# A transformer block on one Trainium2 core: weight parts in two of five pairs of scores instead of two of three

## The chip, the cores and the metric

The kernel runs on one core of one Trainium2 chip. The time is the device time of one execution in microseconds (us); where several runs are told of, it is their median. The engines are PE (matrix multiplication; PEld is its weight load), ACT (exponentials and other functions), DVE (vector work), POOL (GpSimd) and SP, which here only issues transfers. Each engine carries out its own instructions in the order of the program and waits where an instruction needs something that is not there yet.

## The reference

The block takes 2048 tokens of width 512, with 32 heads of width 16 that share one key and one value head, and a gated feed-forward part of width 1792, all in float32.

```python
q = (layernorm(x) @ wq) as 32 heads;  k = layernorm(x) @ wk;  v = layernorm(x) @ wv
h = x + concat_heads(softmax(q k^T / 4) v) @ wo
out = h + (gelu(layernorm(h) @ w_gate) * (layernorm(h) @ w_up)) @ w_down
```

## The kernel before, in words

Accuracy comes from splitting: each float32 matrix is held as a high part and a low part, and a product is three matrix products. The weights `wo`, `w_gate`, `w_up` and `w_down` are split once, during the attention, and the two parts go to DRAM, from where the feed-forward part loads them for each of the four blocks of 512 tokens.

**The scores.** Attention runs over the 4 blocks of tokens; a block has 8 groups of 4 heads, and a group has 16 chunks of 128 keys. For one chunk of one group there are two *scores* (`scores`, L382, called by `score`, L1008): each is two matmuls (L394) into one PSUM tile and one exponential on ACT over 128x1024 (L398). The program counts scores with `n`: 32 to a group, 256 to a block. Two scores with even and odd `n` make a pair; each pair also lets `weigh` (L400) multiply an earlier chunk's exponentials with the values (L402) into the accumulator `acc` of the group. When a group is done, `evacuate` (L413) copies `acc` to `oT` on DVE (L415), SP stores it to DRAM (L419, `acc_d`), and loads it back in another order (L428, `oc`); DVE inverts and multiplies it (L442, L445) and splits it (L453, L457). The queries of the next group are loaded by SP from `q_d` (L374, `qg`) once the current group is at its third chunk.

**Block 0** is written by hand in a loop of its own: `while n < 2 * KC` (L1044) for the first group, `n` from 0 to 31, and `while n < lead` (L1056) for the rest, `n` from 32 to 271, two scores a turn. It has two side works. The first is the queries of the rest of block 0 and of blocks 1 to 3 (`project_q`, L187, called through `later_q`, L306): two or four half matmuls (L392) go beside the scores of a pair; when a group of 128 query columns is done, DVE takes it out of PSUM (L119, L120; a short copy `mark`, L210, stands between its two halves), and SP stores it to `q_d` (L245, three transfers). After four of these the bound of the scores follows: DVE takes the largest norm (L260, L261, into `q`), POOL works out two factors (`factors`, L265: four small operations into `mm`, L266 to L275) two turns later, DVE makes `m` from them (L282) two turns after that, and SP stores `m` (L286).

**The weight parts** are the second side work (`part_weights`, L489, a generator with 46 steps: 4 of `wo`, then for each of 14 columns one of `w_gate`, one of `w_up` and one of `w_down`). I number them 0 to 45. A step issues, in this order: the store of the part before it (POOL's queue, L508 or L514, 512 KB), the load of the part three ahead (SP's queue, L497, 256 KB, into one of four buffers `raw`), and on POOL the split of its own part (`part_f`, L500: a cast, L119, and a subtraction, L120, both over 128x512; for `w_down` a multiplication, L503, ahead of them) into one of two buffers `both`. So a cast waits for its load and for the store of the part two before it, and a load waits until POOL has done with the part four before the one that is loaded.

The engines PE, POOL, ACT, SP and DVE all keep the order in which the program issues here. That order decides what an SP transfer or a POOL operation stands behind. Steps 0 to 3 are taken in the first group (L1052). All others are taken at L1094, at the end of a turn.

At `n` = 256 the loop takes what is left of the weight parts (L1067), closes the buffers of the early stage, and loads `wo` on POOL's queue (L564). From `n` = 272 on the feed-forward work of block 0 is woven between the scores of block 1, and so on; the last block's comes behind all scores.

Of the kernel before, what the change touches and what calls it, by code (L numbers as in the profile page):

```python
# [52 lines left out]
def kernel(  # L53
# [96 lines left out]
    def attend(first):  # L150
        with ExitStack() as outer:
            with tc.manual_schedule(
                engines={mybir.EngineType.PE, mybir.EngineType.Pool, mybir.EngineType.Activation}
            ):
                run(outer, first)


    def run(outer, first):
# [147 lines left out]
        def later_q():  # L306

            second = project_q(1, range(DC), nc.vector, 1, (0, 1))
            for _ in range(sum(RAMP.values())):
                yield next(second)  # L310

            next(q_rest)
            for _ in range(2 * DC - sum(RAMP.values())):
                yield next(second)
            yield from q_rest
            yield 0
            yield from second
            for b in range(2, NB):
                yield from project_q(b, range(DC), nc.vector, b, ())

        def age():
            for entry in after:
                entry[0] -= 1
            while after and after[0][0] <= 0:
                after.pop(0)[1]()
# [83 lines left out]
        def take_out():  # L409
            for step in outs.pop(0):  # L410
                step()
# [148 lines left out]
        def load_wo(b):  # L560

            for j in range(DC // 2):
                w = db.tile([P, 2, 2, D], F32R, tag="w2", bufs=W2, name=f"wo_{b}_{j}")
                (nc.sync if b else nc.gpsimd).dma_start(  # L564
                    w.bitcast(F32),
                    wo_d[2 * j : 2 * j + 2].rearrange("c p i d -> p c i d").bitcast(F32),
                )
                wos[b, 2 * j], wos[b, 2 * j + 1] = w[:, 0], w[:, 1]
# [416 lines left out]
        def finish(n):  # L985
            for _ in range(min(n, len(pend))):
                pb, pg, pkc, pp, pacc, _ = pend.pop(0)
                weigh(pacc, pp, pkc)
                if pkc == KC - 1:
                    evacuate(pb, pg, pacc)  # L990
# [17 lines left out]
        def score(n, beside=()):  # L1008

            nonlocal acc  # L1010
            i, u = divmod(n, 2)
            b, r = divmod(i, PER)
            g, kc = divmod(r, KC)
            if u == 0:
                if kc == 0:
                    cur["qg"] = qgs.pop((b, g))
                    acc = pss.tile([P, T], F32, tag="acc", bufs=1, name=f"acc_{b}_{g}")
                if kc == 2 and b * NG + g + 1 < NB * NG:
                    key = divmod(b * NG + g + 1, NG)
                    qgs[key] = load_q(*key)  # L1020
                cur["p"] = sb.tile([P, 4, T], F32, tag="p", bufs=PB, name=f"p_{i}")
            scores(i, cur["p"], cur["qg"], kc, u, beside)
            if u == 1:
                pend.append((b, g, kc, cur["p"], acc, n))
# [12 lines left out]
        n, lead = 0, 2 * PER + sum(SIZES[: LEAD[0]])  # L1037
        with tc.manual_schedule(engines={mybir.EngineType.SP, mybir.EngineType.DVE}):
            parts, said = None, 3 if first else 0
            if first:  # L1040
                work = later_q()
                parts = part_weights(early.enter_context(tc.tile_pool(name="parts", bufs=1)))

            while n < 2 * KC:  # L1044
                for _ in range(RAMP.get(n, n > 7 and n % 4 == 3) if said else 0):
                    said = next(work)
                    age()
                score(n)
                n += 1
                if n % 4 == 0:  # L1050
                    finish(len(pend) - 2)
                    if parts is not None and n > 12 and n % 24:  # L1052
                        next(parts)

            token, left = next(work) if first else None, 6 * (NB * DC - 2 - DC) * DC
            while n < lead:  # L1056
                age()
                rest = token == REST
                count = 0
                if token is not None and not rest:  # L1060
                    count = min(4 if left > LAST_Q - n else 2, token[1] + 1)
                    left -= count
                if n == 2 * PER:
                    assert token is None
                    while after:
                        age()
                    for _ in parts or ():  # L1067
                        pass
                    if first:
                        check_bound(eb, k2m)  # L1070
                    parts = work = None
                    early.close()
                    db = late.enter_context(tc.tile_pool(name="dense", bufs=1))
                    load_wo(0)
                for j in range(2):
                    if j >= 2 - count // 2:
                        tokens = token, next(work)
                        score(n, [(lane, step) for lane, _, step in tokens])
                        token = next(work, None)
                    else:  # L1080
                        score(n)
                    n += 1
                if n == 2 * PER + 4:
                    primed = dense(0)
                    next(primed)
                if rest:
                    token = next(work, None)
                if len(pend) > 2:
                    finish(1)
                while squares:  # L1090
                    squares.pop(0)()
                if outs and n % 4 == 0:
                    take_out()
                if parts is not None and n % 6:  # L1094
                    next(parts, None)
            assert n == lead
        assert not outs
# [339 lines left out]
    def check_bound(sb, k2m):  # L1437
        q2m = sb.tile([H, 1], F32, name="q2m")
        nc.vector.tensor_reduce(q2m, q2, axis=AX.X, op=ALU.max)
        nc.vector.tensor_tensor(q2m, q2m, k2m, op=ALU.mult)  # L1440
        nc.sync.dma_start(b_d.rearrange("o h -> h o"), q2m)
# [77 lines left out]
```

## Time and profile before

| | us |
|---|---|
| median of 3 runs (lowest, highest) | 1479.35 (1477.3, 1481.3) |
| the profiled execution's own time | 1478.19 |
| its span | 1476.5 |
| PE busy | 1407.0 (95%) |
| ACT busy | 1045.6 (71%) |
| DVE busy | 542.4 (37%) |
| POOL busy | 200.5 (14%) |
| mean granted clock of PE | 0.98 |

How to read it: the profile is one execution. A strip of 40 digits shows the busy tenths of 40 equal slices of the span, 36.9 us each. A timeline merges neighbouring instructions of one kind into a row: start, duration, engine, line, what is written from what, how many (x), and in brackets the idle time ahead of it and what ended that. A table by stretches gives the busy time of each engine between two times, the granted clock of PE and the mean share of the transfer engines that was busy. Rows of SP are issues of transfers, not the transfers themselves.

### The profile page before, as it was taken

The numbers are of one execution on the slowest core, as the hardware profiler recorded it, in microseconds if no ns is written. First come the engines' busy times: TensorE is split into PE (matmuls) and PEld (weight loads), VectorE is DVE, ScalarE is ACT, GpSimd is POOL, SyncE is SP. The second block draws the span as 40 slices with busy tenths as digits, with TensorE's granted clock in tenths as the row PEclk, the third lists the DMA queues.
The fourth block names the chain that finished last, engine by engine and source line by source line (L and its number), as shares of the span: only waits on it lengthen the run. The fifth ranks groups of instructions, "written<-read, shape, count | busy, mean of one in ns | idle before, by whom it ended". The sixth has DMA issues, their size and how long they took to land.

```text
span 1476.5 us, 25577 instructions
## 1 busy us (share of the span) xinstructions
PE 1407.0 (95%) x10622; PEld 778.5 (53%) x10622; DVE 542.4 (37%) x974; ACT 1045.6 (71%) x1149; POOL 200.5 (14%) x286
## 2 busy tenths in 40 slices
PE   9997972899999999999999999999999999999998
PEld 7532320233456565555555555555555555557886
DVE  7411310221345243343334242422344242426665
ACT  7696962799778777777777777777778777773000
POOL 6267766300000000000000000000000000002000
PEclk9998986899999999999999999999999999999999
DMA  4577777424224223223334142405144131426462
GB/s 152 170 230 232 242 228 236 147 80 150 78 79 145 102 97 126 83 83 110 113 102 148 60 155 69 140 27 183 41 162 139 40 133 58 155 91 216 164 211 70
DMA packets 84700, 193.69 MB, mean 131 GB/s; under 512 B 9676, under 2 KB 24012, under 8 KB 84544
## 3 DMA queue, kind: packets, MB, share of 16 engines
q1 hardware_dynamic: 77208, 165.65, 33.6%
q0 software_dynamic: 7200, 26.22, 4.6%
q8 instruction: 85, 1.39, 0.4%
q14 instruction: 39, 0.32, 0.1%
q10 hardware_dynamic: 168, 0.10, 0.0%
HBM read 142.12 MB, written 49.55 MB: 130 GB/s over the span
## 4 chain that ended last, share of the span: by engine, by line
PE 78%; DMA 10%; POOL 5%; ACT 3%; issue 2%; DVE 1%; SPq 1%; POOLq 0%; DVEq 0%; ACTq 0%
PE acc L402 26%; PE s L394 16%; PE pu L913 8%; PE pg L913 7%; PE pd L913 4%; PE pd L590 3%; PE pd L612 3%; PE pg L612 3%; PE pu L612 3%; ACT p L398 2%; DMA w_d<-w_0b 2%; PE pp L590 2%; DMA w_d<-w_1b 1%; POOL w_1b L120 1%; PE pp L721 1%
## 5 line engine op out<-in xcount | busy, mean ns | idle before, releaser
L398 ACT ACTIVATE p<-s 128x1024 f32<-128x1024 f32 x1024 | 974.1, 1029 | 288.4 <-PE s L394 286.7
L402 PE MATMUL acc<-p,v_sb 128*32 128x512 f32 x4096 | 500.9, 602 | 8.9 <-DVE oT L415 8.9
L394 PE MATMUL s<-qg,kaug 50*128 50x512 f32 x1984 | 423.6, 429 | 11.8 <-DMA qg<-q_d 8.1
L394 PEld LDWEIGHTS s<-qg,kaug 50*128 50x128 f32 x1984 | 192.8, 185 | 267.6 <-ACT p L398 157.8
L402 PEld LDWEIGHTS acc<-p,v_sb 128*32 128x32 f32 x4096 | 107.9, 109 | 235.5 <-issue 221.5
L913 PE MATMUL pg<-x2h,w 64*128 64x512 f32 x672 | 211.5, 391 | 0.9 <-DVE mark_pg L936 0.9
L913 PE MATMUL pu<-x2h,w 64*128 64x512 f32 x672 | 212.2, 391 | 0.0
L913 PEld LDWEIGHTS pg<-x2h,w 64*128 64x128 f32 x672 | 116.0, 185 | 15.2 <-DVE mark_pg L936 1.8
L913 PEld LDWEIGHTS pu<-x2h,w 64*128 64x128 f32 x672 | 115.8, 185 | 15.3
L913 PE MATMUL pu<-x2l,w 64*128 64x512 f32 x336 | 121.9, 391 | 0.0
L913 PE MATMUL pg<-x2l,w 64*128 64x512 f32 x336 | 121.9, 390 | 0.0
L790 ACT ACTIVATE ga<-ga 128x512 f32<-128x512 f32 x56 | 35.3, 634 | 89.2 <-DVE ga L785 89.2
L129 POOL TENSOR_SCALAR rstd<-mv 128x1 f32<-128x1 f32 x16 | 3.6, 222 | 682.6 <-DVE mv L127 682.6
L913 PE MATMUL pd<-w,gh 64*128 64x512 f32 x384 | 81.2, 392 | 0.0
L855 DVE TENSOR_TENSOR h<-h,pd 128x512 f32<-128x512 f32 x48 | 31.9, 684 | 115.4 <-PE pd L913 66.3
L442 DVE RECIPROCAL oc<-oc 128x128 f32<-128x128 f32 x64 | 56.3, 921 | 47.9 <-DMA oc<-acc_d 43.3
L1146 DVE SCALAR_TENSOR_TENSOR ga<-ga,g 128x512 f32<-128x512 f32 x70 | 48.3, 690 | 52.6 <-ACT ga L790 51.5
L392 PE MATMUL pq<-xT_hi,wq_hi 64*128 64x512 f32 x80 | 33.6, 419 | 34.6 <-DVE mark L210 33.7
L774 DVE COPY g<-pg 128x512 f32<-128x512 f32 x56 | 38.7, 692 | 63.9 <-PE pg L913 58.2
L913 PEld LDWEIGHTS pu<-x2l,w 64*128 64x128 f32 x336 | 57.9, 185 | 7.4
L913 PEld LDWEIGHTS pg<-x2l,w 64*128 64x128 f32 x336 | 58.0, 185 | 6.9
L415 DVE COPY oT<-acc 128x512 f32<-128x512 f32 x32 | 22.1, 691 | 97.6 <-PE acc L402 97.4
(258 smaller groups left out, 1451.5 us busy)
## 6 DMA issues: line engine op xcount, KB each, us to landing
w<-w_d SPq DMA_DIRECT2D x112, 512.0 KB
w<-w_d SPq DMA_DIRECT2D x28, 1024.0 KB
qg<-q_d SPq DMA_DIRECT2D x48, 200.0 KB
q_d<-qh SPq DMA_DIRECT2D x32, 256.0 KB
acc_d<-oT SPq DMA_DIRECT2D x31, 256.0 KB
oc<-acc_d SPq DMA_DIRECT2D x124, 64.0 KB
w_d<-w_0b POOLq DMA_DIRECT2D x14, 512.0 KB, 6.1
w_d<-w_1b POOLq DMA_DIRECT2D x14, 512.0 KB, 4.8
```

Of the source, the lines that this page charges most:

```text
L392: step()
L394: nc.tensor.matmul(s[:, a, :], kaug[rows, kc * P : (kc + 1) * P], qg[rows, 2 * u + a, :], start=True, stop=True,)
L398: nc.scalar.activation(p[:, 2 * u : 2 * u + 2, :], s, AF.Exp, scale=SCALE)
L402: nc.tensor.matmul(acc[32 * j : 32 * j + 32, :], v_sb[:, kc, :], p[:, j, :], start=(kc == 0), stop=(kc == KC - 1), skip_group_check=True,)
L442: nc.vector.reciprocal(oc[:, 1, sl], oc[:, 1, sl])
L590: nc.tensor.matmul(banks[k], lhsT[rows], rhs[rows], start=(turn == 0 and i == 0), stop=(turn == 1 and i == n - 1), skip_group_check=True,)
L612: nc.tensor.matmul(bank, lhsT, rhs, start=(i == 0), stop=(i == len(ts) - 1))
L774: nc.vector.tensor_copy(g, pg)
L790: nc.scalar.activation(a, a, AF.Tanh, scale=GELU_A * GELU_C)
L855: nc.vector.tensor_tensor(hs[t], hs[t], pd, op=ALU.add)
L913: nc.tensor.matmul(e["bank"], lhsT[rows], rhs[rows], start=i == 0 and not e["both"], stop=last and e["both"], skip_group_check=True,)
L1146: (soon or lazy).pop(0)()
```

## The change

One line is changed, in the loop that issues scores 32 to 271 (L1094):

```diff
-                if parts is not None and n % 6:
+                if parts is not None and n // 2 % 5 in (0, 2):
                     next(parts, None)
```

`n` is even there. Before, a step was taken in every turn whose `n` is no multiple of 6, two turns of three: step 4 at `n` = 34, steps 5 and 6 at 38 and 40, 7 and 8 at 44 and 46, and so on to step 45 at `n` = 158; the last store follows at 160. Now a step is taken in two turns of five: step 4 at `n` = 34, 5 and 6 at 40 and 44, 7 and 8 at 50 and 54, and so on to step 45 at `n` = 240; the last store follows at 244.

The instructions of PE, ACT and DVE are the same and in the same order. On POOL the weight parts and their stores keep their order, and two sets of four `mm` operations stand at other places among them: the set of block 1 now stands behind the split of part 9 (before: 12), that of block 2 behind the split of part 26 (before: 42). That of block 3 still stands behind the last part. On SP the weight loads move back among the stores to `q_d`, `m` and `acc_d` and the loads `oc` and `qg`: the last one, of part 45, now stands just ahead of the store of group 6's `acc` (counted from 0), where before it stood ahead of group 4's. Ahead of the store of group 2's `acc` stand the loads up to part 19; before it were those up to part 28.

## The prediction

> **What bounds the kernel now.** I read the strips of the page first. (Differences under 0.3% of the time, 4.4 us, count as no change here: about what a measurement of this kernel can tell.)
>
> ```profile
> PE   9997972899999999999999999999999999999998
> POOL 6267766300000000000000000000000000002000
> PEclk9998986899999999999999999999999999999999
> ```
>
> PE is busy from end to end, except in slices 3, 5 and 6 (111 to 258 us), and these lie in block 0, in the stretch where POOL splits the weights. The clock falls there too. Next, ACT's timeline through block 0. It holds the scores alone, so the x counts give `n`: the first row is `n` = 32, the second 66, the last 242.
>
> ```profile
> 85.63 1.94 ACT L398 ACTIVATE p<-s 128x1024 f32<-128x1024 f32 x2 [0.43 <-PE s L394]
> ...
> 122.73 3.86 ACT L398 ACTIVATE p<-s 128x1024 f32<-128x1024 f32 x4 [0.20 <-PE s L394]
> 135.97 1.94 ACT L398 ACTIVATE p<-s 128x1024 f32<-128x1024 f32 x2 [9.38 <-PE s L394]
> 138.53 24.77 ACT L398 ACTIVATE p<-s 128x1024 f32<-128x1024 f32 x26 [0.62 <-PE s L394]
> ...
> 202.29 1.94 ACT L398 ACTIVATE p<-s 128x1024 f32<-128x1024 f32 x2 [9.18 <-PE s L394]
> 205.73 15.21 ACT L398 ACTIVATE p<-s 128x1024 f32<-128x1024 f32 x16 [1.51 <-PE s L394]
> 221.72 10.49 ACT L398 ACTIVATE p<-s 128x1024 f32<-128x1024 f32 x11 [0.78 <-PE s L394]
> 266.07 1.03 ACT L398 ACTIVATE p<-s 128x1024 f32<-128x1024 f32 x1 [33.86 <-PE s L394]
> 268.72 1.94 ACT L398 ACTIVATE p<-s 128x1024 f32<-128x1024 f32 x2 [1.62 <-PE s L394]
> 271.77 9.27 ACT L398 ACTIVATE p<-s 128x1024 f32<-128x1024 f32 x10 [1.11 <-PE s L394]
> ...
> 350.73 22.11 ACT L398 ACTIVATE p<-s 128x1024 f32<-128x1024 f32 x24 [0.55 <-PE s L394]
> ```
>
> Three standstills are to be seen, at `n` = 70, 128 and 157: 9.38, 9.18 and 33.86 us. The clean pace is read from the last two rows: 82 scores (`n` = 160 to 241) in 78.96 us, 0.963 us each. DVE's timeline says what the third one waits for.
>
> ```profile
> 220.85 0.67 DVE L261 TENSOR_REDUCE q<-qn 32x1 f32<-32x512 f32 x1
> ...
> 263.91 0.78 DVE L282 TENSOR_SCALAR m<-qn,mm 32x512 fp32r<-32x512 f32 x1 [22.16 <-POOL mm L275]
> 264.62 0.13 DVE L210 COPY mark<-pq 128x1 f32<-128x1 f32 x1
> ```
>
> DVE has `q` at 221.52, but POOL delivers `mm` only at about 263.9: its four operations stand behind the split of part 42. `m` waits for them, `mark` waits behind `m` on DVE, PE waits for `mark` before its next half matmul, and the scores stand behind that. The first standstill is the same in small.
>
> ```profile
> 113.34 0.67 DVE L261 TENSOR_REDUCE q<-qn 32x1 f32<-32x512 f32 x1
> 118.86 0.16 DVE L210 COPY mark<-pq 128x1 f32<-128x1 f32 x1 [4.84 <-PE s L394]
> 131.78 0.78 DVE L282 TENSOR_SCALAR m<-qn,mm 32x512 fp32r<-32x512 f32 x1 [12.76 <-POOL mm L275]
> 132.48 0.67 DVE L415 COPY oT<-acc 128x512 f32<-128x512 f32 x1
> ```
>
> Here `oT` stands behind `m`, and the next group's accumulator behind `oT`. The second one is SP's:
>
> ```profile
> 165.77 0.68 DVE L415 COPY oT<-acc 128x512 f32<-128x512 f32 x1
> ```
> ```profile
> 180.92 1.49 SPq L419 DMA_DIRECT2D acc_d<-oT  x1
> 189.41 1.73 SPq L428 DMA_DIRECT2D oc<-acc_d  x4
> 191.24 0.39 SPq L497 DMA_DIRECT2D w_1r<-in_B_w_up_dram  x1
> 191.73 0.80 SPq L374 DMA_DIRECT2D qg<-q_d  x2
> ```
>
> `oT` is there at 166.45, and its store is issued at 180.92, 14.5 us late, since the loads up to part 28 stand ahead of it and wait for POOL to free their buffers. So the queries of `n` = 128 are issued at 191.73, just before they are wanted. All three come from one thing: POOL is behind its weight parts.
>
> **The change part by part.** It adds and removes no instruction. Each of steps 5 to 45 (an SP load, two or three POOL operations, a POOL store) moves back: step 5 from `n` = 38 to 40, step 45 from 158 to 240. First, can POOL keep this pace?
>
> ```profile
> 89.22 0.60 POOL L119 CAST w_0b<-w_0r 128x512 fp32r<-128x512 f32 x1 [2.83 <-DMA wo_d<-wo2b]
> ...
> 91.49 0.57 POOL L508 DMA_DIRECT2D w_d<-w_0b  x1 [0.30 <-POOL w_0b L120]
> ...
> 114.68 1.29 POOL L120 TENSOR_TENSOR w21b<-w21r,w21b 128x512 fp32r<-128x512 f32 x1
> ...
> 189.80 1.27 POOL L120 TENSOR_TENSOR w_1b<-w_1r,w_1b 128x512 fp32r<-128x512 f32 x1
> ...
> 274.20 0.63 POOL L514 DMA_DIRECT2D w_d<-w213b  x1 [0.30 <-POOL w213b L120]
> ```
> ```profile
> L119 POOL CAST w_1b<-w_1r 128x512 fp32r<-128x512 f32 x14 | 8.5, 609 | 24.9 <-DMA w_d<-w23b 5.3 <-DMA w_d<-w26b 5.0 <-DMA w_d<-w20b 5.0
> ```
> ```profile
> w_d<-w22b POOLq DMA_DIRECT2D x1, 512.0 KB, 3.0
> w_d<-w23b POOLq DMA_DIRECT2D x1, 512.0 KB, 8.7
> ```
>
> Parts 4 to 45 take from 89.22 to 274.83: 185.6 us for 42, 4.42 each, waits for the buffers included (24.9 us of them before one kind of cast, mostly for the store two parts earlier, which lands after 3.0 to 8.7 us). Before, two parts were wanted in six scores, 3 x 0.963 = 2.89 us a part at the clean pace, so POOL fell behind by 1.5 us with each. Now two are wanted in ten scores, 5 x 0.963 = 4.82 us a part. That is 0.4 us more than POOL needed, so it no longer falls behind, with 8% to spare. (POOL and SP may also run up to three parts ahead, as far as loads are issued.)
>
> The standstills, one by one, with times after the change T(n) = 122.73 + 0.963 (n - 66):
>
> - `n` = 70: `mm` now stands behind part 9, whose subtraction ended at 115.97 even before (the `w21b` row). `q` is there at 114.01 and the four operations take some 1.6 us, so `m` finds them at about 118 and runs right behind `mark` at 119. `oT` no longer waits. Gone: 9.38 us.
> - `n` = 128: the loads up to part 19 stand ahead of the store. I keep the slow landing of before, 8.5 us from `acc_d` to `oc` (180.92 to 189.41). `oT` is there 1 us behind T(100) = 155.5; 156.5 + 8.5 + 1.7 + 0.9 puts the queries' issue at about 168; before, the first score came 10.6 us behind that issue (191.73 to 202.29). 179 is 3 us ahead of T(128) = 182.4. Gone: 9.18 us.
> - `n` = 157: `mm` stands behind part 26, whose subtraction ended at 191.07 before (the `w_1b` row at 189.80), ahead of the new T(146) = 199.8 where `q` comes. `m` runs at about 202.5; PE came to need `mark` at `n` = 157, T = 210.4. Gone: 33.86 us.
>
> Behind each standstill stands a restart: 2 scores in 2.56 us (135.97 to 138.53), 2 in 3.44 (202.29 to 205.73), 3 in 5.70 (266.07 to 271.77), against 1.93, 1.93 and 2.89 at the clean pace: 0.63 + 1.51 + 2.81 = 4.95 us, gone too. **The sum:** 9.38 + 9.18 + 33.86 + 4.95 = 57.4 us. As a check: from 122.73 to 350.73 are 176 scores in 228.0 us; at 0.963 they take 169.5, that is 58.5 less.
>
> What is late next: PE itself, whose clean stretch has it without idle time. `n` = 32 to 65 stays as it is (34 scores in 37.1 us, 1.09 each; no standstill in it, and PE carries more half matmuls there). If the parts slow that stretch, up to 34 x (1.09 - 0.963) = 4.3 us more can be had; I take 0.
>
> What the moved steps now lie beside: the last weight parts run until `n` = 244, and two things come behind them on POOL's queue, `mm` of block 3 and the loads of `wo`.
>
> ```profile
> 357.83 1.51 POOL L564 DMA_DIRECT2D wo<-wo_d  x2 [5.34 <-PE s L394]
> ```
> ```profile
> 379.13 0.73 PE L590 MATMUL pp<-wo,o_hi 64*128 64x512 f32 x4 [0.25 <-DMA qg<-q_d]
> ```
>
> The load was issued at 357.83 and its first use came 21 us later. POOL on time is done by T(244) + 4.4 = 298.5, 7 us ahead of T(256) = 305.7, where the loads are due; I cost this at nothing. Without that cover it costs what POOL is behind beyond 7 us and beyond whatever of the 21 us the transfer leaves. `m` of block 3 is covered the same way: it would hold DVE, whose next work is the copy of an `acc` that PE ends at T(259).
>
> The moved POOL work also meets other DVE work:
>
> ```profile
> 268.32 1.65 DVE L457 TENSOR_TENSOR o_lo<-oc,o_hi 128x512 fp32r<-128x512 f32 x1
> ```
> ```profile
> 330.21 0.69 DVE L457 TENSOR_TENSOR o_lo<-oc,o_hi 128x512 fp32r<-128x512 f32 x1
> ```
>
> The same subtraction took 1.65 us while POOL split weights and 0.69 when POOL was idle. The third column of `oc` (the row at 330.21) now falls beside POOL work: about 1 us for each of its three operations, 3 us on DVE. DVE has waits of 4.8 us and more there, so I take 0, and 3 us as the other end. The Trainium skill, "SBUF — State Buffer", section "Who interferes with whom", says that a DVE instruction with two inputs in SBUF and a POOL instruction that reads SBUF exclude one another; the pair of rows agrees with it, and by that rule alone, with nothing hidden, the sum would be some 3 us smaller.
>
> The profiled execution took 1478.19 us; less 57.4 is 1420.8. The median of the runs shown is 1.2 us over it, so the forecast for a median is **1422 us**.
>
> **The rivals.**
>
> *POOL stays a little behind.* For: 8% is little, and where a store lands only after 8.7 us, one turn through the two buffers takes about 2.9 us of POOL work (`w_0b`, from its cast at 89.22 to the end of its store's issue at 92.06) and 8.7 us, 11.6 us for two parts, against 9.6 of pace. Against: only part of the stores land so late. One of the two short standstills then stays, or some 10 us of the long one: 1422 + 10.7 = about 1433. Half of the long one: 1422 + 18 = 1440.
>
> *The transfers bind.* The same bytes move in 57 us less.
>
> ```profile
> 85.50:126.60 41.10, 38.99 (x292) 15.04 (x288) 6.55 (x12) 36.80 (x38) 24.96 (x29) 1.00 0.81 258
> ...
> 271.80:348.20 76.40, 76.16 (x560) 25.55 (x558) 15.02 (x25) 75.59 (x80) 2.57 (x4) 1.00 0.27 88
> ```
>
> The share of busy transfer engines (the last number but one) was 0.81 in a stretch without standstill and 0.27 behind the weights, so there is room to spread into. If landings grow by half all the same, SP is late at two of the six groups, some 5 us each: 1432.
>
> *Slower.* The weights come too late for block 1: POOL is behind at `n` = 256, the loads of `wo` stand behind it, and PE stands at `n` = 273. The price is POOL's lateness less its cover of 7 us (more, if the load has slack of its own). Against a gain of 57.4 it decides from 64 us of lateness on, 42 parts at 4.82 + 64/42 = 6.35 us each; measured are 4.42, and even 11.6 us for every two parts, all stores at their slowest, is 5.8. At 6.5 us a part the time is 1479 + 42 x 0.15 = about 1486.
>
> *It does nothing.* The standstills would stay with other causes (`mark` waiting for something other than `mm`). The rows above speak against it: 1479.
>
> **How the numbers follow.** Forecast, all three gone (1414 to 1428): 0.74. One short standstill or landings that grow (1428 to 1440): 0.16. More than that but faster (1440 to 1475): 0.04. Nothing (within 4.4 us of 1479): 0.02. Slower: 0.04. The lower end is 1422 less 4.3 for the first stretch and less 1.1 for the check, with 2.6 for a clean pace lower by 0.015 over 176 scores: 1414. The upper end takes in the first rival with one standstill, and its half: 1438. Faster by over 0.3%: 0.94; within: 0.02; slower: 0.04.
>
> **What would show it right or wrong.** In ACT's timeline of the changed kernel no gap over 3 us from `n` = 32 to 255, `n` = 242 at about 292 us and `n` = 256 at about 306. DVE's `m` waits less than 2 us for `mm` each time. SP issues `acc_d` within 3 us of `oT`. POOL's last store is issued near 295, and its casts wait less. PE's clock is 1.00 throughout block 0. Behind `n` = 272 all intervals are as before. The forecast is wrong if a gap stays at `n` = 70, 128 or 157, if a new one stands at another group's first score, or if PE waits for `wo` near `n` = 273.

## The result, and the profile after

| | before | after |
|---|---|---|
| median (lowest, highest), 4 runs each, us | 1479.15 (1477.3, 1481.3) | 1426.7 (1419.79, 1428.0) |
| the profiled execution's own time | 1478.19 | 1426.9 |
| its span | 1476.5 | 1425.1 |
| PE busy | 1407.0 (95%) | 1402.1 (98%) |
| mean granted clock of PE | 0.98 | 0.997 |

The ratio is 0.9635 (95% interval 0.9602 to 0.9669): faster by 3.7%. The forecast was 1422, its range 1414 to 1438. The single times after are of two kinds, of the same kernel: one of the four is 1419.79, three are 1426.49 to 1428.0. The profiled execution is one of the longer ones.

First the strips of the page after. Slices are now 35.6 us.

```profile
PE   8999999998999999999999999999999999999998
POOL 6365666620000000000000000000000000002000
PEclk9999999999999999999999999999999999999999
```

The holes in slices 3, 5 and 6 are gone, and with them the dips of the clock in block 0 (a strip of slices is too coarse for the short dip told of below). POOL does the same work (the weight parts reach one slice further), at an even pace. In the chain that ended last (the page's fourth part) DMA had 10% and POOL 5% of the span before; now it reads

```profile
PE 91%; ACT 3%; DVE 2%; DMA 2%; issue 1%; SPq 0%; POOL 0%; DVEq 0%; ACTq 0%; POOLq 0%
```

ACT's timeline after, the first row starts at `n` = 66, the second at 242:

```profile
122.74 7.63 ACT L398 ACTIVATE p<-s 128x1024 f32<-128x1024 f32 x8 [0.20 <-PE s L394]
...
292.89 29.44 ACT L398 ACTIVATE p<-s 128x1024 f32<-128x1024 f32 x32 [0.55 <-PE s L394]
323.29 1.94 ACT L398 ACTIVATE p<-s 128x1024 f32<-128x1024 f32 x2 [0.96 <-PE s L394]
329.17 1.94 ACT L398 ACTIVATE p<-s 128x1024 f32<-128x1024 f32 x2 [3.94 <-PE s L394]
335.80 4.89 ACT L398 ACTIVATE p<-s 128x1024 f32<-128x1024 f32 x5 [4.69 <-PE s L394]
```

`n` = 66 starts at 122.74 as before, `n` = 242 at 292.89 where it was 350.73: 57.84 us gained, and no gap up to there is over 0.8 us. But some of the gain is given back right behind block 0. From `n` = 274 on the gaps are 0.96, 3.94 and 4.69 us. The chain that leads to them is read from four engines: SP, DVE, PE, and the table by stretches (PE busy, PEld, DVE, ACT, POOL, then the granted clock, the share of busy transfer engines, GB/s).

```profile
302.47 1.86 SPq L550 DMA_DIRECT2D w<-w_d  x4
309.09 0.32 SPq L419 DMA_DIRECT2D acc_d<-oT  x1
319.04 1.73 SPq L428 DMA_DIRECT2D oc<-acc_d  x4
```
```profile
322.79 3.39 DVE L442 RECIPROCAL oc<-oc 128x128 f32<-128x128 f32 x4 [13.73 <-DMA oc<-acc_d]
```
```profile
327.42 1.22 PE L590 MATMUL pp<-wo,o_hi 64*128 64x512 f32 x4 [3.29 <-DVE o_hi L453]
329.85 5.42 PE L402 MATMUL acc<-p,v_sb 128*32 128x512 f32 x32
```
```profile
325.00:330.00 5.00, 2.58 (x14) 1.64 (x18) 3.15 (x6) 1.06 (x2) 0.00 (x0) 0.67 0.00 0
330.00:335.00 5.00, 5.00 (x32) 1.07 (x28) 0.00 (x0) 1.10 (x2) 0.00 (x0) 0.65 0.00 0
```

The store of the last group's `acc` is issued the moment `oT` is there, but stands behind the loads for block 1 that were issued 6.6 us before it. `oc` can follow only when the store has landed: 319.04 - 309.09 = 9.95 us. The same two rows before:

```profile
366.92 0.32 SPq L419 DMA_DIRECT2D acc_d<-oT  x1
373.14 1.73 SPq L428 DMA_DIRECT2D oc<-acc_d  x4
```

That was 6.22 us. So `oc` is inverted late, PE stands 3.29 us for `o_hi`, and its clock falls: the means of 0.67 and 0.65 over the two stretches come from a granted clock of 0.50 from 326.7 to 333.5 (the same table in steps of 0.2 us). The 32 matmuls of L402 (two rows up) take 5.42 us; before they took

```profile
383.55 3.64 PE L402 MATMUL acc<-p,v_sb 128*32 128x512 f32 x32
```

From `n` = 272 to 280 the scores took 11.5 us before and 17.4 after: 5.9 us lost. The account of the profiled executions is 57.8 - 5.9 = 51.9; the times differ by 1478.19 - 1426.9 = 51.3.

### The profile page after: what moved, and what is told of

Its sections match the earlier page's. It is cut to its first block, busy times and chain, and to the rows that moved or that the text cites. A ratio compares the mean times of both kernels' runs of the same rounds, so it can differ in the third digit from the quotient of the medians.

```text
span 1425.1 us, 25577 instructions
## 1 busy us (share of the span) xinstructions
PE 1402.1 (98%) x10622; PEld 777.5 (55%) x10622; DVE 541.8 (38%) x974; ACT 1045.1 (73%) x1149; POOL 200.1 (14%) x286
## 4 chain that ended last, share of the span: by engine, by line
PE 91%; ACT 3%; DVE 2%; DMA 2%; issue 1%; SPq 0%; POOL 0%; DVEq 0%; ACTq 0%; POOLq 0%
PE acc L402 32%; PE s L394 20%; PE pu L913 9%; PE pg L913 7%; PE pd L913 4%; PE pd L590 3%; PE pd L612 3%; PE pg L612 3%; PE pu L612 3%; PE pq L392 2%; ACT p L398 2%; PE pp L590 2%; DMA acc_d<-oT 1%; PE pq L204 1%; PE pp L721 1%
## 5 line engine op out<-in xcount | busy, mean ns | idle before, releaser
L402 PE MATMUL acc<-p,v_sb 128*32 128x512 f32 x4096 | 499.3, 601 | 0.0
L402 PEld LDWEIGHTS acc<-p,v_sb 128*32 128x32 f32 x4096 | 107.9, 109 | 227.5 <-issue 222.4
L442 DVE RECIPROCAL oc<-oc 128x128 f32<-128x128 f32 x64 | 56.3, 921 | 33.9 <-DMA oc<-acc_d 29.2
L787 DVE TENSOR_TENSOR g<-g,pu 128x512 f32<-128x512 f32 x56 | 38.4, 685 | 40.6 <-PE pu L913 30.6
```

The lines of the kernel that those rows point to most:

```text
L402: nc.tensor.matmul(acc[32 * j : 32 * j + 32, :], v_sb[:, kc, :], p[:, j, :], start=(kc == 0), stop=(kc == KC - 1), skip_group_check=True,)
L442: nc.vector.reciprocal(oc[:, 1, sl], oc[:, 1, sl])
L787: nc.vector.tensor_tensor(g, g, pu, op=ALU.mult)
```

## The experiments

Two theories went in, each with a rival. **One debt:** all three standstills of before, and nothing else of block 0, come from POOL being behind its weight parts, and what decides is the pace that the program asks for (2.89 us a part before, 4.82 after) against what POOL can do (some 4.4). The rival says that buffers, stores or loads bind, so that the saving turns up as other waits. **B, the order on SP:** the 5.9 us come from the store of the last `acc` standing behind block 1's loads. Its rival, **A**, lays them to the last weight parts, which now end only 16 us ahead of `n` = 256. Ratios are to the kernel before, with 95% intervals.

### The pace of before, but the four small operations leave POOL

```diff
 def factors(...):            # the sets of blocks 1 to 3
-    nc.gpsimd.tensor_scalar(mm...)     # and three more
+    nc.vector.tensor_scalar(mm...)     # the power becomes a multiplication by 0.0
...
-                if parts is not None and n // 2 % 5 in (0, 2):
+                if parts is not None and n % 6:
```

> The kernel before, with its pace of two parts in three pairs, but the four small operations behind `q` run on DVE instead of POOL, for blocks 1 to 3. Their inverse root is left out (the factors are set to zero), so the bound that is taken off the scores is zero there. Theory (one debt): POOL is behind its weight parts by about 1.5 us with each, and the two standstills at n = 70 and 157 are where `m` meets that debt. With `mm` off POOL's queue these two go, but the loads on SP stay tied to POOL, and PE now comes earlier to the groups whose queries stand behind them: about 10 to 15 us at n = 128 and 12 to 18 us at n = 160, time 1440 to 1455 us. Rival (three separate waits): the standstills at 70 and 157 go with their restarts, 46.7 us, the one at 128 stays at 9 us and no other comes: 1432 us.

Measured: 1454.05 us, ratio 0.9828 (0.9809 to 0.9848). The first standstill is gone, the second and third are these (ACT's timeline; lines stand 7 higher here):

```profile
200.02 1.94 ACT L405 ACTIVATE p<-s 128x1024 f32<-128x1024 f32 x2 [17.24 <-PE s L401]
...
241.58 1.02 ACT L405 ACTIVATE p<-s 128x1024 f32<-128x1024 f32 x1 [10.72 <-PE s L401]
```

`m` finds its factors at once, so what is left is the other way in which POOL's lateness reaches PE: through SP, whose weight loads wait for POOL's buffers, with the stores and loads of the attention behind them. DVE and SP show it for the second of the two gaps:

```profile
205.81 0.69 DVE L422 COPY oT<-acc 128x512 f32<-128x512 f32 x1 [1.40 <-PE acc L409]
...
237.65 1.76 DVE L449 RECIPROCAL oc<-oc 128x128 f32<-128x128 f32 x2 [16.59 <-DMA oc<-acc_d]
```
```profile
227.95 0.77 SPq L426 DMA_DIRECT2D acc_d<-oT  x1
232.97 2.04 SPq L435 DMA_DIRECT2D oc<-acc_d  x4
```

`oT` is there at 206.50 and its store is issued at 227.95, 21.4 us late. DVE waits 16.59 us for `oc`, with `m` behind that. The same holder is in the kernel before, and the prediction had not named it: ahead of the wait of `m` for `mm` that it quotes, DVE's timeline there has

```profile
239.99 1.76 DVE L442 RECIPROCAL oc<-oc 128x128 f32<-128x128 f32 x2 [18.46 <-DMA oc<-acc_d]
```

So DVE stood in `oc` until 240, and then in `m` for `mm` until 263.9. It is one debt with two ways to PE: this edit closes the first way and gives 25 us of the 52. The theory's sum held (27.96 us, expected 22 to 33), its two terms less so: the gap at `n` = 128 is larger than the 10 to 15 us expected, and the other one, smaller than 12 to 18 us, is at `n` = 157 in place of 160.

### Other paces

```diff
-                if parts is not None and n // 2 % 5 in (0, 2):
+                if parts is not None and n % 6 == 0:              # one in three
+                if parts is not None and n // 2 % 7 in (0, 2, 4): # three in seven
+                if parts is not None and n % 4 == 0:              # one in two
```

One in three, 5.78 us a part:

> The changed kernel with a weight part in one pair of three (5.8 us a part) instead of two in five. By n = 256 steps 4 to 40 are taken, and five parts are left over and issued at once. Theory: the pace only matters as long as it is slower than POOL's 4.4 us a part, so block 0 has no standstill up to n = 256; then POOL is some 20 us late with the rest, the loads of `wo` stand behind it, and PE stands at about n = 273 to 280 for 15 to 28 us: 1435 to 1455 us. Rival (the lateness is covered by the 16 scores up to n = 272 and the slack of the loads): 1420 to 1428 us, no gap over 6 us.

Three in seven, 4.49 us a part:

> The changed kernel with weight parts in three pairs of seven (4.5 us a part): the last part is taken at n = 228 instead of 240. The changed kernel has a residual of about 6 us at n = 273 to 279, where PE waits for the last column of `oc`. Theory A (the tail of the weight stores): the stores of the last parts, issued up to 7 us before the last stores to `q_d`, hold these up, the buffers of the early stage come free 2 us later, and so do all loads of block 1; with the last weight store some 12 us earlier the residual goes: 1419 to 1422 us, gaps at n = 276 and 278 of about 1 and 3 us as before the change. Rival B (the store of `acc` stands behind the four loads of weights on SP's queue, whenever they start): the residual stays, 1425 to 1428 us. In both, no standstill within block 0, though POOL has no time to spare (4.49 us against 4.42).

One in two, 3.85 us a part:

> The changed kernel with a weight part in every second pair (3.85 us a part). Theory (POOL with its waits needs 4.4 us and more, so it runs into debt again): `mm` of block 2 stands behind part 32 and comes 8 to 17 us too late for PE at n = 157; SP is late too, so that one of the groups at n = 128 or 160 waits: 1430 to 1442 us. Rival (POOL's own work, 3.45 us a part, is what counts, and the waits shrink once the pace is slower): no standstill over 2 us in block 0, 1419 to 1427 us.

| us wanted a part | median | ratio (interval) | standstills of the scores |
|---|---|---|---|
| 2.89 (before) | 1479.15 | 1 | 52.4 in block 0 |
| 3.85 (one in two) | 1440.7 | 0.9742 (0.9724 to 0.9761) | 17.4 at `n` = 157 |
| 4.49 (three in seven) | 1425.93 | 0.9636 (0.962 to 0.9652) | 5.0 at `n` = 157 |
| 4.82 (after) | 1426.7 | 0.9635 (0.9602 to 0.9669) | none in block 0; 5.9 behind it |
| 5.78 (one in three) | 1448.71 | 0.9792 (0.9769 to 0.9815) | none in block 0; 27 behind it |

One in two has the third standstill at half its size (ACT: 17.44 us); the wait at `n` = 128 or 160 that was expected beside it did not come. DVE names the cause as before:

```profile
226.41 0.77 DVE L282 TENSOR_SCALAR m<-qn,mm 32x512 fp32r<-32x512 f32 x1 [19.14 <-POOL mm L275]
```

Three in seven still has 5.02 us of it, though 4.49 is more than the 4.42 of the prediction, and against what was expected of this run:

```profile
215.97 1.02 ACT L398 ACTIVATE p<-s 128x1024 f32<-128x1024 f32 x1 [5.02 <-PE s L394]
...
330.35 3.77 ACT L398 ACTIVATE p<-s 128x1024 f32<-128x1024 f32 x4 [0.93 <-PE s L394]
336.96 4.91 ACT L398 ACTIVATE p<-s 128x1024 f32<-128x1024 f32 x5 [2.83 <-PE s L394]
```
```profile
214.05 0.53 DVE L282 TENSOR_SCALAR m<-qn,mm 32x512 fp32r<-32x512 f32 x1 [12.10 <-POOL mm L275]
```

`mm` stands behind part 28 here, and POOL needs 4.9 us a part up to there (parts 4 to 28, 89.74 to 212.30). In the kernel before it did the same parts in 4.37 us each (89.22 to 198.39). What is new is that POOL waits for loads, 13.1 us in this stretch, where before it waited for none. The longest of these waits, and its load on SP:

```profile
179.01 1.49 POOL L503 TENSOR_SCALAR w25r<-w25r 128x512 f32<-128x512 f32 x1 [9.09 <-DMA w25r<-in_B_w_down_dram]
```
```profile
164.42 1.89 SPq L428 DMA_DIRECT2D oc<-acc_d  x4
167.22 0.36 SPq L497 DMA_DIRECT2D w25r<-in_B_w_down_dram  x1
```

At the slower pace the load of this part (number 21) stands behind `oc` on SP, and `oc` waits 8.57 us from the issue of its store at 155.85. So the slower pace itself costs POOL time: the lateness runs from SP to POOL here, and not only from POOL to SP. The loss behind block 0 is gone here (0.93 and 2.83 us, where after has 0.96, 3.94 and 4.69): A's sign, but the time that A gave is not reached, since the 5 us are lost at `n` = 157 instead. This run alone does not separate A from B: its loads for block 1 have a longer lead as well (307.22 to the store's issue at 316.18, 9.0 us; after, 6.6).

One in three is the slower rival of the prediction in small, with a second wait behind it. POOL's queue, SP and ACT:

```profile
325.42 0.63 POOL L514 DMA_DIRECT2D w_d<-w213b  x1 [0.30 <-POOL w213b L120]
329.21 1.45 POOL L564 DMA_DIRECT2D wo<-wo_d  x2 [3.17 <-DMA w_d<-w213b]
```
```profile
331.76 0.45 SPq L419 DMA_DIRECT2D acc_d<-oT  x1
343.65 1.73 SPq L428 DMA_DIRECT2D oc<-acc_d  x4
```
```profile
341.46 1.02 ACT L398 ACTIVATE p<-s 128x1024 f32<-128x1024 f32 x1 [17.93 <-PE s L394]
...
353.70 1.94 ACT L398 ACTIVATE p<-s 128x1024 f32<-128x1024 f32 x2 [9.12 <-PE s L394]
```

Block 0 is as good as after (`n` = 242 at 294.09), but the parts left over at `n` = 256 are all taken there. The last store is issued at 325.42 and the loads of `wo` wait for it, which is the first gap, 17.93 us. The loads of block 1 on SP wait as well, until 328.88, and the store of the last `acc` stands behind them: `oT` is there at 310.25, the store is issued at 331.76, and `oc` follows 11.9 us later. PE then waits 8.43 us for `o_hi`, which is the second gap, 9.12 us. Together they are 27 us.

### The store of `acc` ahead of block 1's loads

```diff
-                if n == 2 * PER + 4:
+                if n == 2 * PER + 8:
                     primed = dense(0)
                     next(primed)
```

The first step of the feed-forward work, which issues the loads of `xb` and of four weight tiles on SP, comes two turns later and so behind the store of the last `acc`. The pace is that of after.

> The changed kernel with the first loads of block 1 (two of x, four of weights, on SP) issued four scores later, so that they stand behind the store of the last `acc` of block 0, its loads `oc` and the next `qg` on SP's queue, instead of ahead of them. Theory B (the store of `acc` stands behind 2.5 MB of loads): `oc` is loaded within 4 us of its store instead of 10, PE does not wait for it at n = 276, 1418 to 1421 us. Theory A (the tail of the weight stores alone, by way of the buffers that come free late): the order on SP changes nothing while the loads of `wo` on POOL's queue still fill the transfer engines: 1424 to 1428 us. If the weights come too late now, PE waits at its first gate matmul, near n = 300.

Measured: 1419.6 us (four runs, 1419.3 to 1420.5), ratio 0.9597 (0.9581 to 0.9613), the fastest of all. SP and ACT:

```profile
309.02 0.34 SPq L419 DMA_DIRECT2D acc_d<-oT  x1
311.09 1.72 SPq L428 DMA_DIRECT2D oc<-acc_d  x4
...
315.18 2.00 SPq L550 DMA_DIRECT2D w<-w_d  x4
```
```profile
323.23 3.77 ACT L398 ACTIVATE p<-s 128x1024 f32<-128x1024 f32 x4 [0.96 <-PE s L394]
329.83 4.89 ACT L398 ACTIVATE p<-s 128x1024 f32<-128x1024 f32 x5 [2.83 <-PE s L394]
```

`oc` follows 2.07 us behind the store instead of 9.95, and the gaps are 0.96 and 2.83: the 5.9 us are back. The weight parts end as late as after (last store at 289.69), so A is out as the sole cause: the order on SP is enough to take the loss away. The same edit at the old pace:

```diff
-                if n == 2 * PER + 4:
+                if n == 2 * PER + 8:
...
-                if parts is not None and n // 2 % 5 in (0, 2):
+                if parts is not None and n % 6:
```

> The kernel before, with its pace, and with the first loads of block 1 issued four scores later, behind the store of the last `acc` of block 0, as in the run that took the residual away. Theory: in the kernel before `oc` came in time, and PE waited for nothing at n = 273; no change, 1477 to 1481 us. Rival (the place of the loads gains by itself): 1472 to 1475 us.

Measured: 1478.34 us (ten runs), ratio 1.0004 (0.9992 to 1.0016). No change: there `oc` was in time without it.

### After, once more

The kernel of after, unchanged, for the two kinds of times.

> The changed kernel itself, once more. Theory (a narrow miss): the 6 us at n = 273 to 279 come when the last `oc` of block 0 lands too late by a few us, so that PE idles for 3 us and then runs at a lower clock; such a miss happens in some executions and not in others: single times of two kinds, 1419 to 1421 and 1425 to 1428 us, with the second kind in most. Rival (a fixed cost of the later weight stores): all between 1425 and 1428 us.

Measured: 1425.37 us (1420.4 and 1424.29 to 1426.69), ratio 0.964 (0.9627 to 0.9654). Over both sets, two executions of nine take 1419.8 to 1420.4 and seven 1424.3 to 1428.0. The profiled one, 1420.4, is of the short kind, and so shows what differs (SP, ACT):

```profile
302.20 1.92 SPq L550 DMA_DIRECT2D w<-w_d  x4
309.94 0.32 SPq L419 DMA_DIRECT2D acc_d<-oT  x1
316.32 1.73 SPq L428 DMA_DIRECT2D oc<-acc_d  x4
```
```profile
324.15 3.77 ACT L398 ACTIVATE p<-s 128x1024 f32<-128x1024 f32 x4 [0.96 <-PE s L394]
330.75 4.91 ACT L398 ACTIVATE p<-s 128x1024 f32<-128x1024 f32 x5 [2.83 <-PE s L394]
```

The store lands in 6.38 us, and the loss is not there. Counted from the issue of block 1's loads, it lands 316.32 - 302.20 = 14.1 us later; in the profile after that was 16.6, before 373.14 - 358.20 = 14.9. The lead of the loads over the store was 7.7, 6.6 and 8.7 us. So of the 3.6 us between the two executions of after, 1.1 are a shorter lead and 2.5 slower transfers; of the 3.7 us between after and before, 2.1 and 1.6. The stretches around the store (after, then this run) show the second:

```profile
305.00:310.00 5.00, 5.00 (x36) 1.37 (x34) 0.69 (x1) 5.00 (x6) 0.00 (x0) 1.00 0.97 315
```
```profile
306.00:311.00 5.00, 5.00 (x36) 1.26 (x36) 0.69 (x1) 5.00 (x7) 0.00 (x0) 1.00 1.02 417
```

The transfer engines are all busy in both, but move 315 GB/s in one and 417 in the other. Why is open. A late end of the weight parts is not the reason by itself: the last store is 3.6 us *later* in the short execution (293.37, after 289.75). But it has a share, by way of the lead. Where the weights end earlier, at both paces between before and after and before itself, the lead is 8.7 to 9.0 us and the store lands in 6.2. (With the four operations on DVE at the old pace the weights end early too, and there it is 8.4 and 8.35 us: slow transfers come without a late end.) In the profile after, SP waits 4.4 us for a store to `q_d` to land before it can issue block 1's loads (before, 0.2), and in the short execution 2.1 us for the last weight store. A names this way; that the weight stores hold up that store to `q_d` is not shown.

### The pace of before with less work a part

```diff
-                if halve:
+                if halve and False:
...
-                if parts is not None and n // 2 % 5 in (0, 2):
+                if parts is not None and n % 6:
```

> The kernel before, with its pace, without the multiplication of `w_down` by one half on POOL (14 operations of 1.5 us, 21 us in all, left out; the feed-forward part comes out twice too large). Theory (POOL's debt in block 0 is the price, whatever it is made of): POOL's 4.4 us a part fall to about 3.9, it reaches `mm` of block 2 some 19 us earlier, and the standstills shrink with it: 1450 to 1462 us. Rival (the waits for the two buffers fill up what is saved, since a store lands only 3 to 9 us after its issue): POOL still needs 4.3 us and more, 1473 to 1480 us.

Measured: 1471.05 us, ratio 0.9947 (0.9928 to 0.9967). The theory failed here and the rival came nearly right. The standstills are 7.82, 6.09 and 31.00 us, where they were 9.38, 9.18 and 33.86:

```profile
135.37 1.94 ACT L398 ACTIVATE p<-s 128x1024 f32<-128x1024 f32 x2 [7.82 <-PE s L394]
...
199.32 1.94 ACT L398 ACTIVATE p<-s 128x1024 f32<-128x1024 f32 x2 [6.09 <-PE s L394]
...
260.65 1.02 ACT L398 ACTIVATE p<-s 128x1024 f32<-128x1024 f32 x1 [31.00 <-PE s L394]
```
```profile
L119 POOL CAST w_0b<-w_0r 128x512 fp32r<-128x512 f32 x14 | 8.6, 617 | 12.2 <-DMA w_d<-w_1b 11.1 <-DMA wo_d<-wo2b 1.0
```

A third of the parts lose a multiplication of 1.5 us, but POOL still takes about 4.3 us a part: what it saves in work it waits, in good part, for stores out of `both`, 12.2 us ahead of this kind of cast (7.4 in the kernel before). Over all casts of these parts the waits for stores grow from 41.7 to 51.3 us, and 7.1 us of waits for a load come in. So the 4.42 us a part are not POOL's work alone; the turn through the two buffers limits it nearly as much. A version with more of these buffers was not tried.

## Why the prediction was right, and where it was not

**What bounds, and the sum.** Right. Three standstills and three restarts were to go, 57.4 us in all; up to `n` = 242, 57.84 went. The first two landmarks held: `n` = 242 at 292.89 (forecast 292), `n` = 256 at 305.8 (306; 292.89 and 14 scores of 29.44 / 32 us). The clean pace held, the first stretch (`n` = 32 to 65) did not move, and the 4.3 us held open for it were not there. The short executions, 1419.8 to 1420.4, are the profiled execution's own forecast, 1420.8, to 1 us.

**That it is one debt of POOL.** Right as far as the runs go, with POOL's waits for its buffers and loads counted in: the standstills shrink as the pace falls and are gone at 4.82. But the third was argued from `mm` alone. It had a second holder, `oc` through SP, for 18.46 us ahead of it. Without `mm`, 17.2 and 10.7 us were left. The sum did not suffer, since the slower pace takes both away.

**The pace and its 8% to spare.** Right in sign, too generous in size. POOL's timeline after, at the split of part 26 and the set of factors for block 2:

```profile
196.11 1.29 POOL L120 TENSOR_TENSOR w_1b<-w_1r,w_1b 128x512 fp32r<-128x512 f32 x1
200.27 0.25 POOL L266 TENSOR_SCALAR mm<-q,k2m 32x1 f32<-32x1 f32 x1 [2.88 <-DVE q L261]
```

Part 26 is done at 197.40 and POOL waits 2.88 us for `q`: that is the whole margin, not the 8.7 us (191.07 to 199.8) that the prediction had by taking the end of part 26 from the trace of before. There POOL ran unpaced. Paced, it follows the scores, and up to part 26 it waits 11.0 us for loads (2.26, 2.30, 2.45 and 3.99), where before it waited for none. At 4.49 us a part the margin was used up, and 5.0 us of standstill came back. `m` itself ran without a wait for `mm` over 2 us, as forecast.

**The casts wait less.** Right for the stores, wrong for the sum, at no cost. Ahead of the kind of cast whose row the prediction quotes:

```profile
L119 POOL CAST w_1b<-w_1r 128x512 fp32r<-128x512 f32 x14 | 8.7, 623 | 25.6 <-DMA w_d<-w22b 5.7 <-DMA w_d<-w20b 5.0 <-DMA w_d<-w210b 3.7
```

These are 25.6 us, before 24.9, but the row mixes two things. Added up over parts 4 to 45 from POOL's timeline, the waits for stores fall from 41.7 to 29.2 us, and 24.9 us of waits for loads come in, since the loads are now issued at the slower pace. The last store is issued at 289.75, forecast near 295.

**Behind `n` = 272 all intervals as before.** This step failed. It cost the hand-over to block 1 at nothing, and sized only what stands behind POOL, the loads of `wo` with their cover of 7 us. That cover held: `wo` is issued at 302.10, and waits for PE, not for a weight part. What was late was another thing on another queue: the store of the last `acc` and the load `oc`, behind the loads of block 1 on SP. Their slack was no larger than what the lead and the speed of those transfers vary by, a few us. It cost 5.9 us in the profiled execution; by their times, seven executions of nine have it. The median shows it: 1426.7 less 5.9 would be 1420.8. The median is inside the range because room was left there for another rival, a standstill that stays in block 0, and not because this cost was seen.

**The third column on DVE.** Cost at 0 to 3 us: 0 was right for block 0, where no gap is over 0.8 us.

**The rivals.** *POOL a little behind* is the kernel three in seven, at 1425.93: with one short standstill of 5.0 us, not 10.7. *The transfers bind* was right in kind, at one place of the six groups and with 5.9 us (it said two of them, 5 us each). *Slower* was not in reach: one in three asks for 5.78 us a part, loses 17.93 us by this very mechanism and 9.12 by the late `oc`, and is still faster than before, as its bound of 6.35 says. (The sum for 6.5 us a part, 1479 + 42 x 0.15, is 1485 and not 1486.)

## What to carry to other kernels

Where side work is issued at a pace fixed in the program and shares in-order queues with the main chain, compare the pace with what the queue can do in that very stretch and at that very pace, since a new pace puts its loads behind other waits (4.37 us a part became 4.9 with three in seven). Asked for too fast, it puts everything behind it late (52 us here), asked for too slowly, it runs into its own deadline (27 us, with what that makes late in turn), and the best of the paces tried lies between. Look for every way by which the late queue reaches the bounding engine; closing one of two gave half. When a main chain speeds up, check small dependent transfers that stand behind large loads on one queue; moving the loads two turns back was worth the remaining 6 to 7 us.

## What the runs showed of the hardware

A store of 256 KB and the load that depends on it were 2.07 us apart when nothing stood ahead of them on SP's queue (the store of `acc` put ahead), and 6.2 to 9.95 us when six loads of block 1 (2 of 256 KB, 4 of 512) had been issued 6.6 to 9.0 us ahead on the same queue.

The transfer engines at full share moved 315 GB/s in one execution and 417 in another of the same kernel, in stretches at the same place of the program.

One wait of PE of 3.29 us was enough to have the clock granted at 0.50 for 6.8 us, and 32 matmuls took 5.42 us in place of 3.64. The clock fell 2.5 us after PE's last matmul had ended (324.12 to 326.7); ahead of the standstill of three in seven it fell after 2.2 us. The Trainium skill, "TensorE: Matmul & The Clock Gate", section "What's actually happening", puts the idle window behind which the clock falls at about 3.4 us, free-running. In these two places it fell sooner, and the measurement decides.
